# Larger score bursts, earlier transposes and an earlier block 1 in a fused attention and feed-forward kernel

## Chip, cores, metric

One NeuronCore of a Trainium2 chip. The metric is the device time of one execution in microseconds (us). The kernel before takes 245.7 us: 245.55 median of the 3 runs known when the prediction was made, 245.72 of 6 runs later.

## The reference

Sliding-window attention with a few global keys and a slope bias, then a gated feed-forward block on its output.

```python
batch, n_heads, seq, head_dim = (4, 8, 768, 64);  n_global, n_local = (8, 96)
scores = scale * (q @ k.T) + bias        # bias: -slope of the head x distance
scores = where(keep, scores, -1e9)       # keep: 8 global keys, or the 96 keys up to the query
a = softmax(scores);  x = (a @ v)        # heads side by side: 3072 tokens x 512
g = x @ w_gate                           # 512 x 1536
out = (g * sigmoid(g) * (x @ w_val)) @ w_out
```

## The kernel before

The 3072 tokens are 8 tiles of 384; block b (a batch entry) is tiles 2b and 2b + 1. The "head" of the program is what runs before the steps below; it does block 0's attention for its first 384 tokens, and "half 1", the other 384, is done during tile 0. The feed-forward work of a tile has 12 steps f. A step is a gate group (gps, 4 matmuls), a value group (vps, 4) and usually one output part (ops, 3 matmuls of the tile before; four parts make one output of 128 rows). Between the gate and value groups and the output stand a tanh (th, ScalarE) and two products (sl and hT, VectorE); an "eviction" is the copy of a finished output out of its PSUM bank. Attention work is slipped in between steps: score bursts (sc), transposes (trs), and values (den and num). TensorE writes PSUM, which has eight banks here: four (a0 to a3) for attention, three (x0 to x2) that gate and value groups take in turn, and o0 for outputs.

```python
def bank(name, dt=FP32):                       # the next of a0..a3
def spare(name, dt=FP32):                      # the next of x0..x2
    tag = state["x"][gv.get("n", 0) % len(state["x"])]
    gv["n"] = gv.get("n", 0) + 1
    return single(name, tag, dt)

def transposes_half(self, half, tr, k_eng, q_eng):      # of one pair of heads
    for st, dst in ((k16, trk), (q16, trq)):
        for j in range(J2):
            for hi in range(2):
                nc.tensor.transpose(dst[...], st[...], ident)
    ...                                         # then the copies out of PSUM (k_eng, q_eng)

def gate_or_val(t, f, which, c0=0):
    ...
    if which == 0:      # ScalarE: th = tanh(dst / 2);  VectorE: sl = (th + 1) * dst
    else:               # VectorE: hT = dst * sl

def out_part(t, i, part):
    ...                                         # 3 matmuls into o0
    if part == 3:
        nc.scalar.mul(out=osb, in_=ops, mul=0.5)            # the eviction of o0
        nc.sync.dma_start(out=out[r0:r0 + 128, :], in_=osb)

def sc(b, *units):                              # a burst: pairs (hp), thirds of the keys (bk)
    ...  pair.scores(bk, ..., [spare("sc") for _ in range(2)] if len(units) == 3 and i == 0
                     else banks("sc"))
# scores: matmuls now; the exponentials (ScalarE) of the first pair now, of the others "later";
# the masks (VectorE, for some GpSimd) later. One "later" item runs before each group.

def first(t, b):
    return {(t, 3): [tr(b, 0), tr(b, 1)],
            (t, 5): [sc(b, (0, 0), (0, 1), (1, 0))],
            (t, 7): [tr(b, 2), tr(b, 3)],
            (t, 8): [sc(b, (1, 1), (2, 0), (2, 1))],
            (t, 9): [sc(b, (3, 0), (3, 1))],
            (t, 10): [va(b, 0, 0)],
            (t, 11, 1): [va(b, 1, 0)]}

def both(t, b):
    n = b + 1
    return {(t, 0): [sc(b, (0, 2), (1, 2), (2, 2)), fetch(n, 0, 1)],
            (t, 5): [sc(b, (3, 2), (0, 0, n), (1, 0, n)), fetch(n, 2, 3)],
            (t, 8): [vas(b, 1)],
            (t + 1, 0): [sc(n, (0, 1), (1, 1), (2, 0))],
            (t + 1, 4): [sc(n, (2, 1), (3, 0), (3, 1))],
            (t + 1, 8): [vas(n, 0)]}

stretches = [                                   # ff(tile, first step, last step, output parts)
    (ff(0, 0, 12), half1),
    (ff(1, 0, 6, (0, 0, 0, 1, 0, 1)) + ff(1, 6, 11, (1,)) + [(1, 11, 5)], first(1, 1)),
    (ff(2, 0, 12, (1,)) + ff(3, 0, 12, (1,)), both(2, 1)),
    (ff(4, 0, 12, (1,)) + ff(5, 0, 12, (1,)), both(4, 2)),
    ...]
```

The softmax here doesn't subtract the row's maximum and nothing guards it: scores larger than these inputs give would overflow.

Of the kernel before, what the change touches and what calls it, by code (L numbers as in the profile page):

```python
# [37 lines left out]
def kernel(  # L38
# [223 lines left out]
    class Pair:  # L262
# [30 lines left out]
        def transposes_half(self, half, tr, k_eng, q_eng):  # L293
            hp = self.hp
            trq, trk = tr
            for st, dst in ((k16, trk), (q16, trq)):
                for j in range(J2):
                    for hi in range(2):
                        nc.tensor.transpose(  # L299
                            dst[64 * hi:64 * hi + 64, 128 * j:128 * j + 128],  # L300
                            st[:, half, 2 * hp + hi, D * j:D * j + D], ident)
            if half == 0:
# [62 lines left out]
        def scores(self, bk, mul_eng, put_off, sc):  # L365
# [30 lines left out]
            if put_off:  # L396
                later.append(exps)
            else:
                exps()
            later.append(mask)  # L400
# [11 lines left out]
    class Quad:  # L412
# [49 lines left out]
        def values(self, half, bank, mul_eng):  # L462
# [10 lines left out]
            def scale_num(side):  # L473
                mul_eng.tensor_mul(self.x_out(half, side), srcs[side], self.rb)  # L474

            def spread():
                self.spread()
                if mul_eng is nc.gpsimd:
                    for side in range(2):
                        scale_num(side)  # L480
# [3 lines left out]
            if mul_eng is not nc.gpsimd:  # L484
                for side in range(2):
                    later.append(lambda side=side: scale_num(side))
# [11 lines left out]
    def both_values(b, half):  # L498
# [23 lines left out]
        later.append(two[1].spread)  # L522
        for side in range(2):
            later.append(lambda side=side: scale_num(nc.vector, 1, side))
# [90 lines left out]
    def p_tr(hp, kt, qt, q_eng):  # L615
        tr = [single("trs", t, FP16)[:, 0:TB] for t in (qt, kt)]
        pairs[0, hp].transposes_half(0, tr, V, q_eng)
# [28 lines left out]
    load_qk(1, 4, 8)  # L646
    for c in range(NCH):
        load_v_rest(1, c)
# [28 lines left out]
    def sc(b, *units):  # L677
        def step():
            for i, (hp, bk, *other) in enumerate(units):
                pair = pairs[b + 1 if other else b, hp]  # L680
                on_vector = pair.b < 2 or bk < 2 or hp % 2 == 0
                pair.scores(bk, nc.vector if on_vector else nc.gpsimd, bool(later),
                            [spare("sc") for _ in range(2)] if len(units) == 3 and i == 0
                            else banks("sc"))
        return step

    def va(b, g, half):
        return lambda: quads[b, g].values(half, bank, nc.vector if b < 2 else nc.gpsimd)
# [7 lines left out]
    def trh(*units):  # L696
        def step():
            ks, qs = single("trs", "o0", FP16), spare("trs", FP16)
            for i, (hp, k_eng, q_eng) in enumerate(units):
                c = slice(TB * i, TB * i + TB)  # L700
                pairs[0, hp].transposes_half(1, [qs[:, c], ks[:, c]], k_eng, q_eng)
# [10 lines left out]
    def fetch(b, *hps):  # L712
        def step():
            for hp in hps:
                pairs[b, hp].transposes_dma()
            if hps[0] > 0:
                turn_ends(b)
        return step

    def first(t, b):  # L720
        return {(t, 3): [tr(b, 0), tr(b, 1)],
                (t, 5): [sc(b, (0, 0), (0, 1), (1, 0))],
                (t, 7): [tr(b, 2), tr(b, 3)],
                (t, 8): [sc(b, (1, 1), (2, 0), (2, 1))],
                (t, 9): [sc(b, (3, 0), (3, 1))],
                (t, 10): [va(b, 0, 0)],
                (t, 11, 1): [va(b, 1, 0)]}

    def both(t, b):

        n = b + 1
        return {(t, 0): [sc(b, (0, 2), (1, 2), (2, 2)), fetch(n, 0, 1)],
                (t, 5): [sc(b, (3, 2), (0, 0, n), (1, 0, n)), fetch(n, 2, 3)],
                (t, 8): [vas(b, 1)],
                (t + 1, 0): [sc(n, (0, 1), (1, 1), (2, 0))],
                (t + 1, 4): [sc(n, (2, 1), (3, 0), (3, 1))],
                (t + 1, 8): [vas(n, 0)]}
# [110 lines left out]
```

## Time and profile before

One profiled execution, cut where TensorE starts the head's first feed-forward matmul, tile 1's first gate group and tile 2's first value group. These starts are read from TensorE's order of time.

| stretch | us |
|---|---|
| start to the head's first feed-forward matmul (block 0's first half) | 15.41 |
| from there to tile 1's first gate group ("tile 0") | 27.97 |
| from there to tile 2's first value group ("tile 1") | 32.54 |
| from there to the end | 167.83 |
| sum | 243.75 |

Busy shares do not help: TensorE is busy 97% before and 96% after. What helps is the distance between starts: 0.65 us for an undisturbed group, and whatever is more is a burst, a mode change or a wait. In lines of the order of time the two numbers in front are start and duration, the brackets at the end hold the idle time before the first instruction and what ended it. A wait that ends before the modelled end of the matmul before it shows in the distance of the starts and not, or not fully, in the brackets.

### The profile page before, as it was taken

Reading aid. Unit: us, or ns where it says so; the run is one execution under the profiler, and the core shown is the slowest. Engines: PE = TensorE matmul, PEld = TensorE weight load, DVE = VectorE, ACT = ScalarE, POOL = GpSimd, SP = SyncE. Lnnn points to the kernel's source line nnn. Section 1 sums busy time; section 2 is a strip of 40 time slices with the busy share of each in tenths; the row PEclk is TensorE's granted clock in tenths of the full one; section 3 lists DMA queues with packets and bytes.
Section 4 is the critical chain, followed back from the end, with each engine's and each line's share of the span. In section 5 each row is a group of like instructions: output and inputs, shape, how many; then the busy total and the mean of one; then the engine's idle time right before and its main releaser. Section 6 shows DMA issues by size and latency. Waiting matters only on the chain.

```text
span 243.8 us, 6052 instructions
## 1 busy us (share of the span) xinstructions
PE 235.8 (97%) x2428; PEld 136.0 (56%) x2428; DVE 167.1 (69%) x358; ACT 129.4 (53%) x291; POOL 96.8 (40%) x117
## 2 busy tenths in 40 slices
PE   7899898999999999999999999999999999999994
PEld 4555565566465556555565556555655565555543
DVE  5676749888886768776786658776785568555510
ACT  6637576868763655356446465367346534333221
POOL 8999674738980000996062252800032213000000
PEclk9999999999999999999999999999999999999999
DMA  7999999999996684699309778951101101110122
GB/s 142 167 190 198 180 206 198 205 154 126 153 121 117 122 144 100 42 157 148 60 3 140 143 142 94 66 70 44 46 0 46 43 0 46 44 41 5 43 88 86
DMA packets 84612, 25.10 MB, mean 103 GB/s; under 512 B 72816, under 2 KB 81640, under 8 KB 84584
## 3 DMA queue, kind: packets, MB, share of 16 engines
q0 software_dynamic: 65296, 14.05, 65.9%
q1 hardware_dynamic: 18728, 10.30, 16.7%
q8 instruction: 19, 0.31, 0.6%
q10 hardware_dynamic: 560, 0.36, 0.5%
q14 instruction: 9, 0.07, 0.1%
HBM read 28.67 MB, written 6.29 MB: 143 GB/s over the span
## 4 chain that ended last, share of the span: by engine, by line
PE 84%; DVE 7%; ACT 3%; DMA 2%; issue 1%; POOL 0%; DVEq 0%; POOLq 0%
PE gps L539 24%; PE ops L568 23%; PE vps L539 23%; PE sc L375 3%; PE num L439 3%; DMA q<-in_q_dram 2%; PE den L439 2%; DVE sl L552 2%; DVE hT L556 2%; PE sc L335 2%; DVE xT L474 1%; ACT at L357 1%; PE trs L273 1%; ACT th L550 1%; PE trs L299 1%
## 5 line engine op out<-in xcount | busy, mean ns | idle before, releaser
L552 DVE SCALAR_TENSOR_TENSOR sl<-th,gps 128x384 f32<-128x384 f32 x94 | 52.0, 553 | 40.1 <-ACT th L550 39.1
L539 PE MATMUL gps<-xT,wg 128*128 128x384 f16 x376 | 76.9, 327 | 0.4
L539 PE MATMUL vps<-xT,wv 128*128 128x384 f16 x376 | 76.5, 326 | 0.6 <-DVE sl L552 0.5
L550 ACT ACTIVATE th<-gps 128x384 f32<-128x384 f32 x94 | 46.7, 497 | 53.5 <-PE gps L539 52.0
L568 PE MATMUL ops<-wo,hT 128*128 128x512 f16 x276 | 72.8, 379 | 0.0
L556 DVE TENSOR_TENSOR hT<-vps,sl 128x384 f16<-128x384 f32 x94 | 52.0, 554 | 7.9
L539 PEld LDWEIGHTS <-wg 128*128 128x128 f16 x384 | 35.1, 98 | 31.2 <-issue 2.3
L539 PEld LDWEIGHTS <-wv 128*128 128x128 f16 x384 | 37.5, 98 | 26.8 <-issue 2.1
L568 PEld LDWEIGHTS <-hT 128*128 128x128 f16 x276 | 26.9, 98 | 23.9
L383 ACT ACTIVATE at<-sc 128x432 f16<-128x432 f32 x72 | 33.1, 539 | 12.2 <-PE sc L375 12.2
L514 POOL TENSOR_TENSOR xT<-ns,rb 128x384 f16<-128x384 f32 x10 | 9.8, 997 | 67.5 <-DVE rb L455 56.5
L171 POOL DMA_DIRECT2D vS<-in_v_dram x28 | 24.7, 896 | 5.3 <-DMA kst<-in_k_dram 3.8
L574 ACT ACTIVATE osb<-ops 128x512 f32<-128x512 f32 x23 | 13.7, 597 | 21.9 <-PE ops L568 21.9
L394 POOL TENSOR_TENSOR at<-at,masks 128x864 f16<-128x864 f16 x4 | 7.3, 1822 | 23.8 <-ACT at L383 19.1
L394 DVE TENSOR_TENSOR at<-at,masks 128x864 f16<-128x864 f16 x20 | 12.1, 604 | 5.4 <-ACT at L383 5.4
L194 POOL DMA_DIRECT2D kst<-in_k_dram x16 | 13.9, 885 | 2.3 <-PE vps L539 1.7
L357 ACT ACTIVATE at<-sc 128x432 f16<-128x432 f32 (+2 forms) x32 | 11.7, 445 | 5.6 <-PE sc L346 5.4
L194 POOL DMA_DIRECT2D qst<-in_q_dram x16 | 13.7, 877 | 0.2 <-issue 0.2
L510 ACT COPY ns<-num 128x384 f32<-128x384 f32 x20 | 8.1, 492 | 7.9 <-PE num L439 7.9
L439 PE MATMUL num<-at,vS 128*32 128x216 f16 (+6 forms) x560 | 11.1, 226 | 0.0
L391 DVE TENSOR_TENSOR at<-at,masks 128x432 f16<-128x432 f16 x24 | 8.1, 378 | 4.1 <-ACT at L383 4.1
L449 DVE STREAM_TRANSPOSE dT<-den 128x384 f32<-128x384 f32 x16 | 9.3, 581 | 1.4 <-PE den L439 0.9
(74 smaller groups left out, 180.2 us busy)
## 6 DMA issues: line engine op xcount, KB each, us to landing
out_dram<-osb SPq DMA_DIRECT2D x23, 256.0 KB
vS<-in_v_dram POOLq DMA_DIRECT2D x24, 120.0 KB, 5.4
wo<-in_moe_w_out_dram POOLq DMA_DIRECT2D x4, 384.0 KB, 10.4
qst<-in_q_dram POOLq DMA_DIRECT2D x16, 96.0 KB, 4.3
kst<-in_k_dram POOLq DMA_DIRECT2D x16, 90.0 KB, 4.9
wg<-in_moe_w_gate_dram POOLq DMA_DIRECT2D x4, 256.0 KB, 7.7
wv<-in_moe_w_val_dram POOLq DMA_DIRECT2D x4, 256.0 KB, 7.7
kst<-in_k_dram POOLq DMA_DIRECT2D x2, 384.0 KB, 12.0
```

Of the source, the lines that this page charges most:

```text
L171: nc.gpsimd.dma_start(out=vSs[b][NG:NG + n, c, :, :], in_=v[b, :, KC * c:KC * c + n, :].rearrange("h p d -> p h d"))
L194: nc.gpsimd.dma_start(out=st[b][p0:p0 + n, h // 2, :, h % 2, :], in_=src[b, h, 0:n * J].rearrange("(t p) d -> p t d", p=n))
L357: nc.scalar.activation(out=at[:, hi, 0:col + n], in_=sc[hi][:, 0:col + n], func=AF.Exp, scale=scale)
L383: nc.scalar.activation(out=at[:, hi, :], in_=sc[hi][:, 0:BANK], func=AF.Exp, scale=scale)
L394: mul_eng.tensor_mul(at, at, m[:, :, o:o + BANK])
L439: nc.tensor.matmul(dst[r, o:o + n], lhsT=ones[:, 0:32] if side is None else vals[:, 4 * g + j, side::2], rhs=pairs[b, 2 * g + j // 2].at[c ...
L539: nc.tensor.matmul(gv[f, which][:, 0:TB], lhsT=w[:, c, 128 * f:128 * f + 128], rhs=x_of(t)[:, c, :], start=(c == 0), stop=(c == NC - 1))
L550: nc.scalar.activation(out=th, in_=dst[:, 0:TB], func=AF.Tanh, scale=0.5)
L552: nc.vector.scalar_tensor_tensor(out=sl, in0=th, scalar=1.0, in1=dst[:, 0:TB], op0=AluOp.add, op1=AluOp.mult)
L556: nc.vector.tensor_mul(hTs[t][:, f, :], dst[:, 0:TB], gv["sl"])
L568: nc.tensor.matmul(ops, lhsT=hTs[t][:, f, 128 * i:128 * i + 128], rhs=wo[:, f, :], start=(f == 0), stop=(f == NFF - 1))
L574: nc.scalar.mul(out=osb, in_=ops, mul=0.5)
```

## The change

Its intent is stated in its own words: "Score bursts of four pairs from the feed-forward banks on; half 1's transposes ahead of copies; two outputs ahead of tile 1; block 1's steps sooner". The core of the diff:

```diff
@@ trh: half 1 of block 0, two pairs at a time (cut)
-            for i, (hp, k_eng, q_eng) in enumerate(units):
-                pairs[0, hp].transposes_half(1, [qs[:, c], ks[:, c]], k_eng, q_eng)
+            for hp, tr in pair_of:
+                pairs[0, hp].turn_half(1, tr)
+            for hp, tr in pair_of:
+                pairs[0, hp].copy_half(1, tr, k_eng, A)
@@ sc: banks and order of the exponentials (cut)
+                where = ([spare("sc"), spare("sc")] if i == 0 and len(units) > 2 else
+                         [single("sc", "o0"), spare("sc")] if i == 3 else banks("sc"))
+            now = [0, 3] if len(units) == 4 else [0]
@@ values of half 1: one scaling to GpSimd
-        return lambda: quads[b, g].values(half, bank, nc.vector if b < 2 else nc.gpsimd)
+        return lambda: quads[b, g].values(half, bank, nc.gpsimd if (b, g, half) == (0, 1, 1) else nc.vector)
@@ first(t, b)
-        return {(t, 3): [tr(b, 0), tr(b, 1)],
-                (t, 5): [sc(b, (0, 0), (0, 1), (1, 0))],
-                (t, 7): [tr(b, 2), tr(b, 3)],
-                (t, 8): [sc(b, (1, 1), (2, 0), (2, 1))],
-                (t, 9): [sc(b, (3, 0), (3, 1))],
-                (t, 10): [va(b, 0, 0)],
-                (t, 11, 1): [va(b, 1, 0)]}
+        return {(t, 2): [tr(b, 0), tr(b, 1)],
+                (t, 3): [sc(b, (0, 0), (0, 1), (1, 0))],
+                (t, 5): [tr(b, 2), tr(b, 3)],
+                (t, 6): [sc(b, (1, 1), (2, 0), (2, 1))],
+                (t, 7): [sc(b, (3, 0), (3, 1))],
+                (t, 8): [va(b, 0, 0)],
+                (t, 10): [va(b, 1, 0)]}
@@ both(t, b)  (second is alike)
+        return {(t, 3): [all_of(b, 2), fetch(n)], (t, 7): [vas(b, 1)], (t, 11): [all_of(n, 0)],
+                (t + 1, 3): [all_of(n, 1)], (t + 1, 7): [vas(n, 0)]}
@@ stretches
-        (ff(0, 0, 12), half1),
-        (ff(1, 0, 6, (0, 0, 0, 1, 0, 1)) + ff(1, 6, 11, (1,)) + [(1, 11, 5)], first(1, 1)),
+        (ff(0, 0, 11) + [(0, 11, 2)], half1),
+        (ff(1, 0, 3) + ff(1, 3, 11, (1,)) + [(1, 11, 2)], first(1, 1)),
@@ loads of block 1: from the head to step 11 of tile 0
+    at_step(0, 11, lambda: load_qk(1, 4, 8), lambda: [load_v_rest(1, c) for c in range(NCH)])
```

Not shown here: at a tile's first step all "later" items were run at once, and now only those up to the last scaling are.

More of the change, by code (lines that the diff above doesn't have):

```diff
@@ L290, in transposes, with turn_half @@
                 in_=k3[:, 0, NG:2 * NG].unsqueeze(1).broadcast_to([128, NCH, NG]))
-        def transposes_half(self, half, tr, k_eng, q_eng):
+        def turn_half(self, half, tr):
             hp = self.hp
@@ L301, in transposes_half, with copy_half @@
                             st[:, half, 2 * hp + hi, D * j:D * j + D], ident)
+        def copy_half(self, half, tr, k_eng, q_eng):
+            trq, trk = tr
+            hp = self.hp
             if half == 0:
@@ L363, in scores_half, with scores @@
                 exps()
-        def scores(self, bk, mul_eng, put_off, sc):
+        def scores(self, bk, mul_eng, sc):
             hp = self.hp
@@ L394, in mask @@
                     mul_eng.tensor_mul(at, at, m[:, :, o:o + BANK])
-            if put_off:
-                later.append(exps)
-            else:
-                exps()
-            later.append(mask)
+            return exps, mask
         def transposes_dma(self):
@@ L473, in scale_num @@
             def scale_num(side):
-                mul_eng.tensor_mul(self.x_out(half, side), srcs[side], self.rb)
+                eng = mul_eng if side else nc.vector
+                eng.tensor_mul(self.x_out(half, side), srcs[side], self.rb)
             def spread():
@@ L478, in spread, with scale @@
                 if mul_eng is nc.gpsimd:
-                    for side in range(2):
-                        scale_num(side)
+                    scale_num(1)
             later.append(lambda: self.invert(den))
             later.append(spread)
-            if mul_eng is not nc.gpsimd:
-                for side in range(2):
-                    later.append(lambda side=side: scale_num(side))
+            for side in range(1 if mul_eng is nc.gpsimd else 2):
+                def scale(side=side):
+                    scale_num(side)
+                later.append(scale)
         def denominators(self, den):
@@ L521, in both_values, with spread, scale @@
         later.append(spread_first)
-        later.append(two[1].spread)
+        def spread():
+            two[1].spread()
+        later.append(spread)
         for side in range(2):
-            later.append(lambda side=side: scale_num(nc.vector, 1, side))
+            def scale(side=side):
+                scale_num(nc.vector, 1, side)
+            later.append(scale)
     hTs = {}
@@ L616, in p_tr @@
         tr = [single("trs", t, FP16)[:, 0:TB] for t in (qt, kt)]
-        pairs[0, hp].transposes_half(0, tr, V, q_eng)
+        pairs[0, hp].turn_half(0, tr)
+        pairs[0, hp].copy_half(0, tr, V, q_eng)
     V, A = nc.vector.tensor_copy, nc.scalar.copy
@@ L645 @@
     load_wo(3)
-    load_qk(1, 4, 8)
-    for c in range(NCH):
-        load_v_rest(1, c)
     p_bias(0, 0, "a0", "a1")
@@ L678, in step @@
         def step():
-            for i, (hp, bk, *other) in enumerate(units):
-                pair = pairs[b + 1 if other else b, hp]
-                on_vector = pair.b < 2 or bk < 2 or hp % 2 == 0
-                pair.scores(bk, nc.vector if on_vector else nc.gpsimd, bool(later),
-                            [spare("sc") for _ in range(2)] if len(units) == 3 and i == 0
-                            else banks("sc"))
+            work = []
+            for i, (hp, bk) in enumerate(units):
+                pair = pairs[b, hp]
+                on_vector = b < 2 or bk < 2 or hp % 2 == 0
+                where = ([spare("sc"), spare("sc")] if i == 0 and len(units) > 2 else
+                         [single("sc", "o0"), spare("sc")] if i == 3 else banks("sc"))
+                work.append(pair.scores(bk, nc.vector if on_vector else nc.gpsimd, where))
+            now = [0, 3] if len(units) == 4 else [0]
+            for i in now:
+                work[i][0]()
+            masks_now = [work[i][1] for i in now]
+            rest = [w for i, w in enumerate(work) if i not in now]
+            for exps, _ in rest:
+                later.extend(masks_now[:1] + [exps])
+                masks_now = masks_now[1:]
+            later.extend(masks_now + [mask for _, mask in rest])
         return step
     def va(b, g, half):
-        return lambda: quads[b, g].values(half, bank, nc.vector if b < 2 else nc.gpsimd)
+        return lambda: quads[b, g].values(half, bank, nc.gpsimd if (b, g, half) == (0, 1, 1) else nc.vector)
     def vas(b, half):
@@ L694, in tr, with trh @@
         return pairs[b, hp].transposes
-    def trh(*units):
+    def trh(h0, h1, by_engine):
         def step():
-            ks, qs = single("trs", "o0", FP16), spare("trs", FP16)
-            for i, (hp, k_eng, q_eng) in enumerate(units):
-                c = slice(TB * i, TB * i + TB)
-                pairs[0, hp].transposes_half(1, [qs[:, c], ks[:, c]], k_eng, q_eng)
+            b0, b1 = single("trs", "o0", FP16), spare("trs", FP16)
+            (a, b), (c, d) = [(t[:, 0:TB], t[:, TB:2 * TB]) for t in (b0, b1)]
+            k_eng = V if by_engine else A
+            pair_of = [(h0, (c, a)), (h1, (d, b))] if by_engine else [(h0, (b, a)), (h1, (d, c))]
+            for hp, tr in pair_of:
+                pairs[0, hp].turn_half(1, tr)
+            for hp, tr in pair_of:
+                pairs[0, hp].copy_half(1, tr, k_eng, A)
         return step
@@ L710, in sch, with fetch, all_of @@
         return step
-    def fetch(b, *hps):
+    def fetch(b):
         def step():
-            for hp in hps:
+            for hp in range(NP):
                 pairs[b, hp].transposes_dma()
-            if hps[0] > 0:
-                turn_ends(b)
+            turn_ends(b)
         return step
     def first(t, b):
-        return {(t, 3): [tr(b, 0), tr(b, 1)],
-                (t, 5): [sc(b, (0, 0), (0, 1), (1, 0))],
-                (t, 7): [tr(b, 2), tr(b, 3)],
-                (t, 8): [sc(b, (1, 1), (2, 0), (2, 1))],
-                (t, 9): [sc(b, (3, 0), (3, 1))],
-                (t, 10): [va(b, 0, 0)],
-                (t, 11, 1): [va(b, 1, 0)]}
+        return {(t, 2): [tr(b, 0), tr(b, 1)],
[5 more added lines that the diff above has]
+                (t, 10): [va(b, 1, 0)]}
+    def all_of(b, bk):
+        return sc(b, *[(hp, bk) for hp in range(NP)])
     def both(t, b):
         n = b + 1
-        return {(t, 0): [sc(b, (0, 2), (1, 2), (2, 2)), fetch(n, 0, 1)],
-                (t, 5): [sc(b, (3, 2), (0, 0, n), (1, 0, n)), fetch(n, 2, 3)],
-                (t, 8): [vas(b, 1)],
-                (t + 1, 0): [sc(n, (0, 1), (1, 1), (2, 0))],
-                (t + 1, 4): [sc(n, (2, 1), (3, 0), (3, 1))],
-                (t + 1, 8): [vas(n, 0)]}
+        return {(t, 3): [all_of(b, 2), fetch(n)], (t, 7): [vas(b, 1)], (t, 11): [all_of(n, 0)],
+                (t + 1, 3): [all_of(n, 1)], (t + 1, 7): [vas(n, 0)]}
     def second(t, b):
-        return {(t, 0): [sc(b, (0, 2), (1, 2))], (t, 3): [sc(b, (2, 2), (3, 2))],
-                (t, 7): [vas(b, 1)]}
-    half1 = {(0, 1): [trh((0, A, A), (1, V, A))], (0, 2): [sch(0)],
-             (0, 3): [sch(1), trh((2, V, A), (3, V, V))], (0, 5): [sch(2)], (0, 6): [sch(3)],
+        return {(t, 3): [all_of(b, 2)], (t, 7): [vas(b, 1)]}
+    half1 = {(0, 1): [trh(0, 1, False)], (0, 2): [sch(0)],
+             (0, 3): [sch(1), trh(2, 3, True)], (0, 5): [sch(2)], (0, 6): [sch(3)],
              (0, 7): [va(0, 0, 1)], (0, 8): [va(0, 1, 1)]}
@@ L793 @@
             if f == 0:
-                run_later(len(later))
+                while any(fn.__name__ in ("spread", "spread_first", "scale") for fn in later):
+                    run_later(1)
             for which in range(2):
```

## The prediction

> **What bounds the kernel now.** I read the page first (engine shares, then the chain that ended last), then the order of time of TensorE alone, then that of all engines around one burst.
>
> ```profile
> PE 235.8 (97%) x2428; PEld 136.0 (56%) x2428; DVE 167.1 (69%) x358; ACT 129.4 (53%) x291; POOL 96.8 (40%) x117
> ...
> PE 84%; DVE 7%; ACT 3%; DMA 2%; issue 1%; POOL 0%; DVEq 0%; POOLq 0%
> ```
>
> TensorE is the bound, but a modelled busy of 97% says nothing about pace, so I use start-to-start times. A gate group (gps), a value group (vps) and an output part (ops) each take 0.65 us when nothing is in the way. From 77 us to the end nearly every group keeps that pace: there only the bursts of attention work cost extra. Two bursts, from TensorE's order of time:
>
> ```profile
> 103.54 0.81 PE L568 MATMUL ops<-wo,hT 128*128 128x512 f16 x3
> 104.29 0.73 PE L375 MATMUL sc<-qT,kT 64*128 64x216 f16 x12
> 104.95 0.82 PE L539 MATMUL gps<-xT,wg 128*128 128x384 f16 x4
> ...
> 190.45 0.81 PE L568 MATMUL ops<-wo,hT 128*128 128x512 f16 x3
> 191.19 0.34 PE L375 MATMUL sc<-qT,kT 64*128 64x216 f16 x4
> ...
> 191.68 0.82 PE L539 MATMUL gps<-xT,wg 128*128 128x384 f16 x4
> ```
>
> From ops to the next gps is 1.41 us with three pairs in between and 1.23 us with two. Without the 0.65 of the ops itself, and with the 0.01 that the next group loses, a burst costs 0.77 or 0.58 us: 0.19 per pair, and 0.2 fixed for entering and leaving.
>
> The stalls lie in the first 77 us. Half 1 of block 0 (the same view):
>
> ```profile
> 18.69 0.36 PE L299 MATMUL trs<-ident,k 128*64 128x128 f16 x6
> ...
> 19.75 0.36 PE L299 MATMUL trs<-ident,k 128*64 128x128 f16 x6 [0.53 <-ACT kT L312]
> ...
> 20.42 0.82 PE L539 MATMUL gps<-xT,wg 128*128 128x384 f16 x4
> ...
> 26.54 0.36 PE L299 MATMUL trs<-ident,k 128*64 128x128 f16 x6 [0.77 <-DVE kT L312]
> ...
> 40.60 0.81 PE L539 MATMUL vps<-xT,wv 128*128 128x384 f16 x4 [0.46 <-DVE sl L552]
> 41.52 0.81 PE L539 MATMUL gps<-xT,wg 128*128 128x384 f16 x4
> 42.45 0.81 PE L539 MATMUL vps<-xT,wv 128*128 128x384 f16 x4
> 43.38 0.81 PE L539 MATMUL gps<-xT,wg 128*128 128x384 f16 x4
> ```
>
> The second pair's transposes wait for the first pair's copies, as both use the same two banks; at the end of tile 0 groups are 0.93 us apart instead of 0.65, because VectorE is busy without a gap from 35 to 43 us. In tile 1 the chain shows 1.70 us of ScalarE (exponentials) at 64.4, between two score bursts one step apart: TensorE goes from 64.38 (ops) to 66.44 (gps), 2.06 us for 0.65 + 0.58, so 0.83 us are lost. Tile 2's first gate group takes 0.95 us (74.98 to 75.93), so it waits 0.3 for its last input.
>
> **What the Trainium skill says.** "TensorEngine Tiling (Array Packing)", Key Properties: "Mode switching requires drain". The trace agrees: that is the fixed 0.2 us. "PSUM — Partial Sum Buffer", the specifications and the section on bank collisions: there are 8 banks, and engines are to be kept apart by bank; the trace shows the waits (0.53 and 0.77 above). "TensorE: Matmul & The Clock Gate", the paragraph on engine queue depths: ScalarE and VectorE are strict FIFO. The trace agrees: no ScalarE work here overtakes another. "ScalarE: Activation LUTs", What ACT_TABLE_LOAD costs: 186 ns + 0.833 ns per element, overlapping by some 93 ns. That gives 546 ns for 432 elements and 612 for 512; the trace has 539 and 597, and four exponentials start 0.41 us apart. I use the trace's.
>
> **The change part by part.**
>
> 1. *Fewer, larger bursts.* From tile 2 on there are 4 + 4 bursts of three pairs and 2 of two; after it 3 + 3 + 1 of four. Before: 8 x 0.77 + 2 x 0.58 = 7.32 us. After: 7 x (0.58 + 2 x 0.185 = 0.95) = 6.65. Gain **0.7**, all on TensorE's path.
>
> 2. *What it pays for that.* Four pairs take all eight banks: the three of gate and value, the four attention banks, and the output bank o0. The burst sits after f = 3 or 11, where the fourth output part has just ended, so ScalarE must first empty o0. All engines around the two-pair burst at 191.19 show what that takes:
>
> ```profile
> 191.29 0.60 ACT L574 ACTIVATE osb<-ops 128x512 f32<-128x512 f32 x1 [0.81 <-PE ops L568]
> ...
> 191.79 0.95 ACT L383 ACTIVATE at<-sc 128x432 f16<-128x432 f32 x2
> ```
>
> With B the burst's start, the eviction runs from B + 0.10 to B + 0.70, and the first pair's exponentials start at B + 0.60. The fourth pair would start at B + 3 x 0.185 = 0.555 and now waits for o0 until 0.74. The next gate group would start at B + 0.855, but its bank in the rotation of three is the first pair's, whose exponential ends at 0.60 + 0.54 = 1.14, so B + 1.18. Loss 1.18 - 0.855 = 0.32 us per burst, x 7 = **2.3 us**. Further on I find no wait: the tanh two steps later slips to about B + 4.3, sl ends at 5.4, and the bank is wanted at 5.7. In the kernel before no output eviction stands just ahead of a three-pair burst, and the next gate bank is one that VectorE frees.
>
> 3. *Transposes ahead of copies.* From 18.60 (the natural end before it) to gps 20.42 is 1.8 us for 24 transposes; 48 transposes in tile 1 run from 49.39 to 50.85, so 24 need 0.8. Gain 0.95 the first time. The second time (25.24 to 27.00) the same 0.95, but the tanh of that step then stands behind two query copies and two exponentials on ScalarE, and the value group after it waits some 0.6 for its bank. Together **1.35**.
>
> 4. *End of tile 0.* One scaling (546 ns, 0.46 from start to start) moves from VectorE to GpSimd, where it takes 997 ns and has time: GpSimd's loads of block 1 now come after it. Two output parts (1.3 us) go between tile 0's last value group and tile 1's first gate group. That last value group comes 1.35 sooner (41.10 for 42.45), the outputs end at 43.05, and tile 1 starts there instead of at 43.38, with 1.3 us of work already done: **1.6 us** ahead, part 3 included.
>
> 5. *Tile 1 sooner.* The work is the same less 1.3 us: 12 x 1.30 + 10 x 0.65 + two transposes of 1.55 + bursts 0.77 + 0.77 + 0.58 + values 2 x 1.0. But the transposes and the first burst are now one step apart instead of two, with mask exponentials on ScalarE in the same steps. Laid out by hand, the first burst waits 0.3 for the sl before it, the burst after the second transposes up to 0.9 (VectorE: two masks, two query copies of 0.95), the 0.83 between the two bursts stays, and tile 2's input comes about 0.75 late, as three output parts fewer cover it. That is 2.8 against 1.1 now, up to 1.7 worse. Such a layout adds up delays that partly fall on top of one another, so I take a fifth to a third of it: **+0.4**.
>
> Loads: the second half of block 1's keys and queries goes out some 3 us later (37.8 to about 41). The DMA queues are full until then and issues wait for earlier ones, so landing moves little: keys landed at 51.0 (37.82 + 13.2), queries at 53.6 (39.80 + 13.8), and they are wanted at about 55.5.
>
> Sum: -0.7 + 2.3 - 1.6 + 0.4 = +0.4, so 246.0. I shade it to **245.4**: the two waits of part 2 are the only large loss, each read from a single other burst, and a schedule that was tuned to end its outputs just before the burst may lose less than my layout says.
>
> **Rivals.** (a) The four-pair bursts are free: o0 and the exponentials come in time. For it: ScalarE is busy only 53%, and from 77 us on nothing waits today. Against: the eviction cannot start before B + 0.10 and takes 0.6. Then the sum is 245.55 - 0.7 - 1.6 + 0.4 = 243.6. (b) The head gains all it lost, without new waits in tile 1: about 3.3 us of stalls in tile 0 and 1.1 in tile 1 vanish, some 242.5 with the bursts free, 244 with them costing. Against: VectorE and ScalarE are the limit there and lose no work but one scaling. (c) ScalarE or VectorE becomes the bound in tile 1, with the full 1.7 us, or the later key loads hold up the second transposes: 247 to 248. For it: VectorE is at 80 to 90% in those slices; against: the average leaves room.
>
> **Range and chances.** The rivals span 242.5 to 248. I give 8 in 10 to 243.3 to 247.3. A gain of over 2% (below 240.6) would need more than all the stalls of the first 77 us, about 4.5 us, and the switches besides: 0.03. A loss of over 2% (above 250.5) would need both extra waits to be double what I find: 0.02. Within 2%: 0.95.
>
> **What would show each step right or wrong.** Part 1: seven score bursts after tile 2 starts, of 16 or 24 matmuls. Part 2: the gate group after each starts about 1.9 us after the ops before it; without the waits it would be 1.6. Its releaser is the exponential, that of the last pair's matmuls the output eviction. Part 3: no wait of transposes for copies; gps at 19.5 and 25.1 where it was 20.4 and 27.0. Part 4: tile 1's first gate group at about 43 with six output matmuls ahead of it. Part 5: waits of TensorE for VectorE and ScalarE between 50 and 75 us, and tile 2's start at 74 to 75.5. I am wrong by over 1 us if the bursts don't wait, or if tile 1 turns bound by ScalarE or VectorE, or waits for its loads.

## The result

The changed kernel takes 248.33 us (median of 6 runs, 247.88 to 249.57); the kernel before took 245.72 (6 runs). The ratio is 1.0104, with a 95% interval of 1.0062 to 1.0147. Ratios here are the mean time of one kernel's fast runs over that of the other's of the same rounds, so not quite the ratio of the medians quoted. The change is 1% slower; "within 2%" held, but the predicted time of 245.4 was 2.9 too low and 248.33 lies above the range.

The same four stretches (the head's first matmul is at 16.51 in this profile):

| stretch | before | after | difference | with the two output parts counted | predicted |
|---|---|---|---|---|---|
| start | 15.41 | 16.51 | +1.10 | | 0 |
| tile 0 | 27.97 | 29.10 | +1.13 | -0.17 (1.30 of outputs done already) | -1.6 |
| tile 1 | 32.54 | 32.80 | +0.26 | +1.56 (1.30 of outputs less) | +0.4 |
| tile 2 to the end | 167.83 | 169.38 | +1.55 | | +1.6 |

The stretch "start" is a difference between executions and not the change: block 0's first queries landed 0.8 us later in this execution, and later runs with the same head code started their feed-forward at 14.8 to 16.0 us. The profiled run was the slowest of its six (249.57). In tile 0 it is rather a lucky one: three further executions with the same code there (a1, a4 and e1 below) have +0.3 to +0.5 where it has -0.17. Without that line the stretches give +2.9, the timed runs +2.6.

The page of the changed kernel, engine shares and chain:

```profile
PE 238.4 (96%) x2428; PEld 137.1 (55%) x2428; DVE 165.1 (67%) x353; ACT 128.4 (52%) x295; POOL 97.5 (39%) x118
...
PE 77%; DMA 6%; ACT 6%; POOL 4%; DVE 4%; issue 2%; DVEq 0%; POOLq 0%
```

TensorE's share of the chain fell from 84% to 77%, and DMA rose from 2% to 6%: a new kind of wait. A four-pair burst with all engines beside it:

```profile
103.80 0.81 PE L576 MATMUL ops<-wo,hT 128*128 128x512 f16 x3
...
104.55 1.11 PE L379 MATMUL sc<-qT,kT 64*128 64x216 f16 x16
104.65 0.60 ACT L582 ACTIVATE osb<-ops 128x512 f32<-128x512 f32 x1 [0.81 <-PE ops L576]
105.14 1.79 ACT L387 ACTIVATE at<-sc 128x432 f16<-128x432 f32 x4
...
105.72 0.82 PE L547 MATMUL gps<-xT,wg 128*128 128x384 f16 x4
```

From the output group to the next gate group it is 1.92 us, the predicted figure, and all seven bursts take 1.91 to 1.93. The eviction starts 0.10 after the burst, and the gate group 1.17 after it (1.18 predicted). The view merges the four pairs; in a window that begins at 105.29 the fourth stands apart:

```profile
105.30 0.36 PE L379 MATMUL sc<-qT,kT 64*128 64x216 f16 x4
```

It starts 0.75 after the burst (0.74 predicted), although a pair takes only 0.19. The semaphores in the packed trace name the releasers that the prediction named: the eviction (osb) for this pair, the exponential (at) for the gate group.

Tile 0 in TensorE's order of time:

```profile
20.59 0.82 PE L547 MATMUL gps<-xT,wg 128*128 128x384 f16 x4
...
22.01 0.50 PE L547 MATMUL vps<-xT,wv 128*128 128x384 f16 x2 [0.28 <-DMA wv<-in_moe_w_val_dram]
...
28.57 0.50 PE L547 MATMUL vps<-xT,wv 128*128 128x384 f16 x2 [0.49 <-DMA wv<-in_moe_w_val_dram]
...
43.67 0.81 PE L547 MATMUL vps<-xT,wv 128*128 128x384 f16 x4 [0.77 <-DVE sl L560]
44.32 1.46 PE L576 MATMUL ops<-wo,hT 128*128 128x512 f16 x6
45.62 0.81 PE L547 MATMUL gps<-xT,wg 128*128 128x384 f16 x4
```

Step 2 (20.59, or 4.08 after the head's first matmul) is 0.93 sooner than before (5.01), as foreseen. But then two value groups wait in their middle for the weights wv (in the packed trace the last wv for steps 4 to 7 landed at 28.53). By step 5 only 0.50 us is left of the 1.46 that TensorE was ahead at step 4, and by step 9 still 0.52. The last value group of tile 0 waits 0.77 for VectorE: it starts 1.57 after its gate group (42.10), where the kernel before had 0.93.

And tile 1, in the same view:

```profile
56.51 0.81 PE L547 MATMUL vps<-xT,wv 128*128 128x384 f16 x4
58.19 0.81 PE L576 MATMUL ops<-wo,hT 128*128 128x512 f16 x3 [0.87 <-ACT osb L582]
...
77.79 0.79 PE L547 MATMUL gps<-xT,wg 128*128 128x384 f16 x2 [0.29 <-DVE xT L475]
```

The output group of step 5 waits for the eviction of the output before: it starts 1.68 after its value group at 56.51, so 1.03 is lost. ScalarE's order of time says why; the eviction stands behind four score exponentials and two mask exponentials:

```profile
55.15 0.37 ACT L252 ACTIVATE masks<-dist 128x216 f16<-128x216 f16 x1
55.42 0.94 ACT L387 ACTIVATE at<-sc 128x432 f16<-128x432 f32 x2
56.24 0.57 ACT L252 ACTIVATE masks<-dist 128x432 f16<-128x432 f16 x1
56.69 0.96 ACT L387 ACTIVATE at<-sc 128x432 f16<-128x432 f32 x2
57.51 0.63 ACT L582 ACTIVATE osb<-ops 128x512 f32<-128x512 f32 x1
```

### The profile page after: what moved, and what is told of

Its sections match the earlier page's. It is cut to its first block, busy times and chain, and to the rows that moved or that the text cites. A ratio compares the mean times of both kernels' runs of the same rounds, so it can differ in the third digit from the quotient of the medians.

```text
span 247.8 us, 6053 instructions
## 1 busy us (share of the span) xinstructions
PE 238.4 (96%) x2428; PEld 137.1 (55%) x2428; DVE 165.1 (67%) x353; ACT 128.4 (52%) x295; POOL 97.5 (39%) x118
## 4 chain that ended last, share of the span: by engine, by line
PE 77%; DMA 6%; ACT 6%; POOL 4%; DVE 4%; issue 2%; DVEq 0%; POOLq 0%
PE gps L547 23%; PE ops L576 23%; PE vps L547 22%; DMA wv<-in_moe_w_val_dram 4%; PE num L439 3%; DMA vS<-in_v_dram 3%; ACT at L387 2%; ACT osb L582 2%; PE den L439 2%; POOL k L119 1%; DVE xT L475 1%; POOL q L119 1%; PE trs L273 1%; POOL wg L213 1%; PE ops L592 1%
## 5 line engine op out<-in xcount | busy, mean ns | idle before, releaser
L558 ACT ACTIVATE th<-gps 128x384 f32<-128x384 f32 x94 | 47.6, 506 | 74.6 <-PE gps L547 73.7
L547 PEld LDWEIGHTS <-wg 128*128 128x128 f16 x384 | 35.6, 98 | 32.6 <-issue 1.7
L379 PE MATMUL sc<-qT,kT 64*128 64x216 f16 (+2 forms) x152 | 10.3, 247 | 0.4 <-ACT at L387 0.2
```

Of the source, the lines that this page charges most:

```text
L547: nc.tensor.matmul(gv[f, which][:, 0:TB], lhsT=w[:, c, 128 * f:128 * f + 128], rhs=x_of(t)[:, c, :], start=(c == 0), stop=(c == NC - 1))
L558: nc.scalar.activation(out=th, in_=dst[:, 0:TB], func=AF.Tanh, scale=0.5)
```

## The experiments

The theory after the result: three separate losses. From tile 2 on, each four-pair burst pays for the bank o0 and for the first exponential (+1.5). In tile 0 the weights land when they always did, so earlier transposes only find a new wait, and the scaling on GpSimd does not relieve VectorE. In tile 1 the eviction stands behind exponentials. The rivals are with each run. Twelve kernels ran, the first eleven timed in five rounds beside the kernel before. Stretches are from one profiled execution of each; "tile 0" counts from the head's first feed-forward matmul, so the start is left out. The kernels built on the changed one, and the run with two outputs ahead, do 1.30 us more of outputs in tile 0 and so much less in tile 1.

| run | median us | ratio to before (95%) | tile 0 | tile 1 | rest |
|---|---|---|---|---|---|
| before | 245.5 to 245.9 | | 27.97 | 32.54 | 167.83 |
| changed | 248.33 | 1.0104 (1.0062 to 1.0147) | 29.10 | 32.80 | 169.38 |
| a1, bursts of three | 247.17 | 1.0049 (1.0006 to 1.0092) | 29.54 | 32.81 | 167.83 |
| a2, no wait for weights | 248.00 | 1.0091 (1.0043 to 1.0140) | 28.59 | 32.81 | 169.36 |
| a3, scaling on VectorE | 247.94 | 1.0090 (1.0046 to 1.0134) | 29.30 | 32.82 | 169.37 |
| a4, masks later | 248.02 | 1.0085 (1.0045 to 1.0124) | 29.79 | 32.10 | 169.36 |
| b1, transposes ahead, alone | 245.46 | 0.9995 (0.9969 to 1.0020) | 27.17 | 32.54 | 167.81 |
| b2, with split weight load | 244.52 | 0.9965 (0.9940 to 0.9990) | 26.93 | 32.55 | 167.82 |
| c1, all mended | 245.65 | 1.0011 (0.9982 to 1.0040) | 27.94 | 32.10 | 167.84 |
| c2, outputs at the end | 244.91 | 0.9980 (0.9951 to 1.0008) | 28.74 | 31.73 | 167.82 |
| d1, b2 and two outputs ahead | 245.33 | 0.9985 (0.9943 to 1.0028) | 28.92 | 31.79 | 167.82 |
| d2, b2 and values first | 245.17 | 0.9965 (0.9931 to 1.0000) | 26.94 | 32.73 | 167.82 |
| d3, d2 and a copy on VectorE | 245.25 | 0.9966 (0.9932 to 1.0000) | 28.17 | 32.74 | 167.82 |
| e1, eviction twice | 253.51, one look | | 29.58 | 32.81 | 173.77 |

The last two stretches repeat to 0.02 us where the code is the same. Tile 0 does not: with the same code it is 29.1 to 29.8, as the weights land sooner or later. The intervals of the timed runs are 0.5 to 1% wide, so for single parts the stretches carry the argument and the timed runs only check its direction.

### a1: bursts of three again

```diff
 # on the changed kernel, from tile 2 on
-        return {(t, 3): [all_of(b, 2), fetch(n)], (t, 7): [vas(b, 1)], ...
+        return {(t, 0): [sc(b, (0, 2), (1, 2), (2, 2)), fetch(n, 0, 1)],
+                (t, 5): [sc(b, (3, 2), (0, 0, n), (1, 0, n)), fetch(n, 2, 3)], ...
```

> The changed kernel with the bursts of block 1's last third and of blocks 2 and 3 put back to three pairs (two in tile 6), at their old places; the rest of the change stays. Theory (each four-pair burst waits 0.19 us for the output eviction and 0.13 us for the first exponential): from tile 2 on the time falls by about 1.5 us, so some 246.8, and groups from tile 2's first value group to the end take 167.9 us again. Rival (the waits are covered, the loss is all in the first 77 us): no change beyond the run-to-run spread, 248.3.

The rest takes 167.83 us again, 1.55 less, to 0.01 as before, and the ratio falls from 1.0104 to 1.0049. The burst in TensorE's order of time:

```profile
104.76 0.81 PE L576 MATMUL ops<-wo,hT 128*128 128x512 f16 x3
...
106.17 0.82 PE L547 MATMUL gps<-xT,wg 128*128 128x384 f16 x4
```

It is 1.41 us for three pairs, against 1.92 for four. So a pair costs (1.41 - 0.65 + 0.01) / 3 = 0.26 us in a burst of three and (1.92 - 0.65) / 4 = 0.32 in one of four: the larger burst is the dearer one, although there are fewer changes between groups and bursts. This run puts back the places of the bursts with their size, so it doesn't separate the two.

### e1: the eviction made twice

```diff
 # on the changed kernel, for the output part just ahead of a four-pair burst
+            for _ in range(2 if gv.get("twice") else 1):
+                nc.scalar.mul(out=osb, in_=ops, mul=0.5)
```

> The changed kernel with the eviction of the output bank just ahead of each four-pair burst made twice (the same result written twice). Theory (part 2 of the prediction: the fourth pair waits for the output bank, and the next gate group for an exponential that stands behind the eviction): a second eviction starts 0.50 us after the first, so from the output group to the next gate group it takes 1.92 + 0.50 = 2.42 us, and from tile 2 on 7 x 0.5 = 3.5 us more than 169.4. Rival (the extra time of a burst is the array's own change of mode or its pace with eight banks): unchanged, 1.92 us.

All engines beside one burst:

```profile
103.98 0.81 PE L576 MATMUL ops<-wo,hT 128*128 128x512 f16 x3
...
106.10 0.36 PE L379 MATMUL sc<-qT,kT 64*128 64x216 f16 x4 [0.65 <-ACT osb L583]
...
106.53 0.82 PE L547 MATMUL gps<-xT,wg 128*128 128x384 f16 x4
```

The fourth pair now waits visibly for the eviction, and the distance is 2.55 us, 0.63 more than with one; the stretch grows by 4.39, which is 7 x 0.63. The expected 0.50 was too small, as the second of these two evictions, of the same bank into the same tile, started 0.63 after the first and not 0.50 (the pair of them took 1.23). With a1 this settles the burst: the eviction of o0 is on its path. The run delays the exponentials too, as they stand behind the eviction, so it doesn't share the 0.32 out between the two; the changed kernel's trace does (the fourth pair starts at 0.75, where it was worked out at 0.56 without the wait; the gate group at 1.17). (This was one look, its state unknown; the clock was 1.0 and only stretches are compared.)

### a2: no wait for weights

```diff
 # on the changed kernel; wrong results on purpose (relative error 0.51)
-                gv[f, which][:, 0:TB], lhsT=w[:, c, 128 * f:128 * f + 128],
+                gv[f, which][:, 0:TB], lhsT=w[:, c, 128 * (f % 2 if t == 0 else f):...],
```

> The changed kernel with wrong results on purpose: every step of tile 0 from the third on multiplies with the first two 128-column blocks of the gate and value weights, which landed long before; all loads are still made. Theory (the transposes put ahead of copies only bring TensorE sooner to weights that land when they always did): the waits for wv in tile 0 go, tile 0's sixth step starts about 1 us sooner (0.9 to 1.3), and the whole falls by 0.5 to 1.2, unless VectorE at the end of tile 0 takes it back. Rival (weights are no limit, the waits for wv are those of a late start of the profiled run): no gain.

The waits for wv are gone, and step 5 starts 11.00 us after the head's first matmul (12.40 in the changed kernel, 12.90 before): 1.40 sooner, a little over the expected 0.9 to 1.3. But TensorE's order of time has another wait a group later, one that the prediction had named (0.6):

```profile
28.00 0.81 PE L547 MATMUL vps<-xT,wv 128*128 128x384 f16 x4 [0.72 <-DVE sl L560]
```

At step 7 the gain over the kernel before is 17.74 - 16.70 = 1.04, where 1.35 was predicted; with the weights' waits, the changed kernel's own profile has 0.53 there, and those of a1, a3 and a4 have 0.09, -0.32 and -0.16. So the weights take 0.5 to 1.4 us of the step's gain. The expected 0.5 to 1.2 of the whole is not seen: the timed ratio, 1.0091, is too close to 1.0104 for a verdict of its own.

### b1 and b2: the transposes alone, and with a split load

```diff
 # b1: on the kernel before, only turn_half / copy_half and the new trh
-    half1 = {(0, 1): [trh((0, A, A), (1, V, A))], ...
+    half1 = {(0, 1): [trh(0, 1, False)], ...
 # b2: b1, and
-    load_w(4, 8)
+    load_w(4, 6)
+    load_w(6, 8)
```

> The kernel before with one part of the change alone: half 1's transposes of two pairs ahead of their copies. Counted from the first matmul of the head's feed-forward, tile 0's step 2 started at 5.01 us before. Theory (weights land when they always did): step 2 starts 0.94 sooner, then TensorE waits for wv and wg, and by step 5 (12.90 before) no more than 0.1 to 0.6 is left; the whole changes by less than 0.6. Rival (the prediction's part 3): step 5 and all after it are 1.35 sooner, 244.4.

> The same with the load of weight columns for steps 4 to 7 of tile 0 made in two halves (steps 4 and 5, then 6 and 7), so that what step 4 needs lands sooner. Theory: the waits for weights at step 4 shrink from 1 us to 0.3 or less, a wait of the value group of step 5 for VectorE's sl of some 0.6 appears instead, as in the run without weight waits; step 5 starts 0.9 to 1.6 sooner than before and the whole falls by 0.7 to 1.1 against the kernel before. Rival (the load path, not the order, is the limit): the same waits as in the run without the split.

In b1 the waits stand in TensorE's order of time for both weights:

```profile
25.73 0.50 PE L543 MATMUL gps<-xT,wg 128*128 128x384 f16 x2 [0.20 <-DMA wg<-in_moe_w_gate_dram]
...
27.13 0.50 PE L543 MATMUL vps<-xT,wv 128*128 128x384 f16 x2 [0.58 <-DMA wv<-in_moe_w_val_dram]
```

The value group's second half starts at 27.13 us, and in the other runs with earlier transposes and no split load at 27.3 to 28.8. In the kernel before it was due at 27.98 and did not wait: it came just behind its weights, which landed at 27.73 by the packed trace. In b1's profile 0.78 us were left at step 5, above the theory's 0.6, and 0.80 at tile 1; that execution was the fastest of its six. The timed runs show no gain (0.9995, interval -0.3 to +0.2%), which agrees with the theory's "less than 0.6" but would not exclude 0.7; the rival's 1.35 is outside.

In b2 both waits are gone, and the same wait for sl as in a2 is left:

```profile
27.76 0.81 PE L543 MATMUL vps<-xT,wv 128*128 128x384 f16 x4 [0.73 <-DVE sl L556]
```

What step 4 needs last landed at 24.80, where it landed at 27.09 in b1. Step 5 starts 1.90 sooner than before, more than the expected 0.9 to 1.6, and step 7 is at 16.69, within 0.01 of the run without any need for weights. So at step 4 the order of the loads was the limit and not the load path. For the whole of tile 0 that isn't shown: of the six kernels with the split load, c2, d1 and d3 waited for weights at other steps in their profiles (0.47 and 0.43; 0.80 and 0.35; 1.21 and 0.42). Tile 0 falls by 1.04, and the time by 0.35% (interval 0.1 to 0.6%): 244.52 us. This is the version that beats both kernels; d2 and d3, built on it, have the same ratio, with intervals that reach 1.

### a3: the scaling back on VectorE

```diff
-        return lambda: quads[b, g].values(half, bank, nc.gpsimd if (b, g, half) == (0, 1, 1) else nc.vector)
+        return lambda: quads[b, g].values(half, bank, nc.vector)
```

> The changed kernel with the one scaling of half 1 that went to GpSimd back on VectorE. Theory (both engines' scalings read two SBUF operands at the same time and VectorE's took 1.19 us instead of 0.54, so nothing was saved): the tail of tile 0 is as long as with GpSimd, within 0.2 us; VectorE's two scalings take 0.54 each. Rival (GpSimd relieves VectorE by 0.46 us, as predicted): 0.4 to 0.5 us slower.

Both sides missed: it is not equal, and the way round is the opposite of the rival. From step 11's gate group to tile 1's first gate group, two output parts included, the changed kernel takes 3.52 us (also in a1, a2 and a4, to 0.01), a3 takes 2.87. GpSimd's help costs 0.65. The two scalings of the changed kernel, all engines:

```profile
41.75 0.99 POOL L475 TENSOR_TENSOR xT<-ns,rb 128x384 f16<-128x384 f32 x1 [4.20 <-DVE rb L455]
41.97 1.19 DVE L475 TENSOR_TENSOR xT<-ns,rb 128x384 f16<-128x384 f32 x1
...
43.08 0.54 DVE L560 SCALAR_TENSOR_TENSOR sl<-th,gps 128x384 f32<-128x384 f32 x1
```

and of a3:

```profile
41.55 0.54 DVE L475 TENSOR_TENSOR xT<-ns,rb 128x384 f16<-128x384 f32 x1
...
42.01 0.54 DVE L560 SCALAR_TENSOR_TENSOR sl<-th,gps 128x384 f32<-128x384 f32 x1
...
42.47 0.55 DVE L475 TENSOR_TENSOR xT<-ns,rb 128x384 f16<-128x384 f32 x1
```

VectorE's scaling takes 1.19 us beside GpSimd's and 0.54 without it. It comes ahead of sl, which in a3 runs between the two scalings, so sl and the bank it frees are 0.65 later. The Trainium skill has this in "SBUF — State Buffer", Who interferes with whom: "A DVE instruction with two SBUF inputs contends with a GpSimd instruction that reads SBUF". The trace agrees, with the two durations above; the prediction had not looked there. In the timed runs a3 has 1.0090, which does not tell it from the changed kernel.

### a4: mask exponentials later

```diff
-    spots = [...] + [(1, f // 2) for f in range(10)]
+    spots = [...] + [(1, f) for f in (0, 0, 1, 1, 2, 2, 5, 5, 6, 6)]
```

> The changed kernel with the mask exponentials of the last pair moved on ScalarE from steps 3 and 4 of tile 1 to steps 5 and 6. Theory (in tile 1's step 5 the output group waits 1.03 us for an eviction that stands behind four score exponentials and two mask exponentials): the wait falls to 0.2 or less and the whole by 0.8 to 1.0. Rival (another wait takes its place, at the burst of step 6 or 7, where ScalarE is busy too): less than 0.3 gained.

The wait for the eviction in TensorE's order of time:

```profile
57.66 0.81 PE L576 MATMUL ops<-wo,hT 128*128 128x512 f16 x3 [0.16 <-ACT osb L582]
```

Its value group starts at 56.68, so 0.33 of the 1.03 is left (0.2 or less expected), and tile 1 takes 32.10 in place of 32.80. That is 0.70, just under the expected 0.8 to 1.0, and no other wait took its place. What still stands ahead of the eviction are the four score exponentials. The timed ratio (1.0085) agrees in direction only.

### c1 and c2: all mended together

```diff
 # c1: a1 + a3 + a4 + the split load of b2, on the changed kernel;  c2: c1, and
-        (ff(1, 0, 3) + ff(1, 3, 11, (1,)) + [(1, 11, 2)], first(1, 1)),
+        (ff(1, 0, 4) + ff(1, 4, 11, (1,)) + [(1, 11, 3)], first(1, 1)),
```

> The changed kernel with what the runs found mended together: bursts of three from tile 2 on (1.5), the scaling back on VectorE (0.6 at the end of tile 0), the last pair's mask exponentials later (0.7), the split weight load (0.5 to 0.9). If the losses add up: 248.3 - 3.3 to 3.7 = 244.6 to 245.0, so some 0.7 to 1.1 below the kernel before. Rival (they overlap): equal to the kernel before within 0.4.

> The same, with the output part after step 3 of tile 1 moved to the end of tile 1, so that three output parts and not two stand between tile 1's last value group and tile 2's first gate group. Theory: tile 2's first gate group waits 0.65 less for its input (0.76 in the changed kernel), and 0.5 to 0.6 comes off. Rival: VectorE is behind by then whatever TensorE does in between, or the burst of step 3 waits instead: no gain.

In c1 each mended stretch is there: 27.94, 32.10 and 167.84, together 0.46 less than before. From the changed kernel's profile the three stretches fall by 3.40, within the expected 3.3 to 3.7, so there the losses do add up. But the timed runs give 1.0011: the 0.7 to 1.1 below the kernel before is excluded, and the rival's "equal within 0.4" fits, though not for its reason, as no overlap is seen. The profiled execution was the fastest of c1's six; what the others lose is not shown. In c2, tile 1 falls by another 0.37 (0.5 to 0.6 expected): no wait for tile 2's input is left, but the burst of step 3 now waits 0.47 for sl, as its rival said. In this execution tile 0 again waited for weights (0.47 and 0.43), in spite of the split. Its 0.998 is not told from 1. What the changed kernel's plan for tile 1 costs shows here even when mended: 31.73 + 1.30 = 33.03 for the same outputs that take 32.54 before.

### d1: two outputs ahead of tile 1, alone

```diff
 # on b2
-        (ff(0, 0, 12), half1),
-        (ff(1, 0, 6, (0, 0, 0, 1, 0, 1)) + ...
+        (ff(0, 0, 11) + [(0, 11, 2)], half1),
+        (ff(1, 0, 6) + ...
```

> The kernel with the transposes ahead and the split weight load (on the order of the kernel before otherwise), and with one more part of the change: two output parts go ahead of tile 1, taken from its steps 3 and 5. Prediction's part 4 without the GpSimd scaling: the wait of some 0.3 us at tile 1's first gate group is filled, so tile 1's first gate group starts 1.0 later with 1.3 us of work done: 0.3 gained. Rival (what tile 1 loses as cover, its steps 3 to 5 then outrun ScalarE and VectorE): the 0.3 is given back or more, tile 1 to tile 2 takes more than 32.54 - 1.30 = 31.24 us.

From step 11 to tile 1's first gate group it takes 2.87 against 1.86 in b2: 1.01 for 1.30 us of work, so the predicted 0.3 is gained. Tile 1 takes 31.79, and 31.25 (b2's 32.55 less 1.30) would be even: 0.54 is given back, as the rival said. Tile 0's own 28.92 is not used here, because this execution waited 0.80 and 0.35 for weights. Against the changed kernel's 32.80 it also shows what the new plan of tile 1 costs: both have ten output parts in tile 1, and the old order takes 1.0 less. This is for block 1's earlier steps and the other places of the outputs together (five at the end of tile 1 in d1, two in the changed kernel).

### d2 and d3: the wait between the two score bursts of tile 1

```diff
 # d2: on b2
-                (t, 9): [sc(b, (3, 0), (3, 1))],
-                (t, 10): [va(b, 0, 0)],
+                (t, 9): [va(b, 0, 0)],
+                (t, 10): [sc(b, (3, 0), (3, 1))],
 # d3: d2, and half 1's last query copy on VectorE
-                pairs[0, hp].copy_half(1, tr, k_eng, A)
+                pairs[0, hp].copy_half(1, tr, k_eng, V if hp == 3 else A)
```

> The same kernel without that part, but in tile 1 the values of the first two pairs are weighed in step 9, between the two score bursts of steps 8 and 10, instead of after the second in step 10. Theory (the second burst waits 0.83 us because its banks are those of the first burst's exponentials, one step before): the wait goes, tile 1 to tile 2 takes about 31.7 instead of 32.54, and the whole is 0.7 to 0.9 below the kernel it is made from, some 243.8. Rival (the values need the same four banks and so wait as long, or the last values then wait for the last pair's masks): less than 0.3 gained.

> The same as the run with values first, and half 1's last query copy goes from ScalarE to VectorE, so that the tanh of tile 0's step 4 stands behind one copy less. Theory (the 0.73 us wait of step 5's value group is ScalarE's order): the wait falls by 0.3 to 0.45 and so does the whole. Rival (VectorE is then the later one): no gain or a loss up to 0.3.

In d2 the burst no longer waits, but the last values do, for the masks of the last pair:

```profile
71.15 0.48 PE L443 MATMUL den<-at,ones 128*32 128x144 f16 x6 [0.78 <-DVE at L395]
```

Tile 1 takes 32.73 (32.55 in b2): the rival was right, the wait only moved. In d3 the 0.73 wait for sl is replaced by 0.27 for the copy on VectorE; from step 4 to step 7 it takes 6.62 us for d2's 7.01, so 0.39 is gained, as expected. But the same profile waits 1.21 and 0.42 for the weights of step 8, and the timed ratio equals d2's (0.9966 and 0.9965). So 0.39 in tile 0 is either lost to the weights or too small to see; this stays open.

## Why the prediction was wrong, point by point

Two steps failed: parts 3 and 4 in tile 0, and the size of part 5 in tile 1. In tile 0 the last value group was to start 1.35 sooner, counted from the head's first feed-forward matmul, and started 0.12 later: 0.83 of that was gone by step 9 (part 3), 0.65 went at the end (part 4). Tile 1 took 1.56 more in place of 0.4.

- **Part 1, fewer bursts, and part 2, what they pay.** Right, in size and in cause. The sum was 2.3 - 0.7 = +1.6; 1.55 was measured, each burst took the predicted 1.92, putting three pairs back gave all of it back, and doubling the eviction lengthened each burst by the time of the second eviction.
- **Part 3, transposes ahead of copies.** This failed. The 0.95 per pair of transposes was right where TensorE waits for copies (0.93 at step 2; step 3 to step 4 takes 3.20 for 4.17). The step "together 1.35" assumed that nothing else was due by then. The weights for steps 2 to 7 were: 0.50 was left at step 5 in the profile, and a2 gives the value without them at step 7 as 1.04, so the tanh wait was also a little larger than the 0.6 stated (step 5 to step 7 takes 5.70 for the 4.84 of before, so 0.86). The prediction checked the landing of block 1's keys, which did not matter, and not that of the weights.
- **Part 4, GpSimd and the outputs ahead.** The outputs ahead gain 0.3, as said (d1). The scaling on GpSimd was to take 0.46 off VectorE, so that the last value group could keep the 1.35 (it is no term of its own in the sum); it costs 0.65. The prediction took GpSimd's 997 ns as free, because that engine was idle; it slows VectorE's own scaling by 0.65.
- **Part 5, tile 1 sooner.** The size was wrong: "a fifth to a third" of a worked 1.7, +0.4, where 1.56 was measured. The reason for the discount, that such delays fall on top of one another, did not hold. The terms were mixed: 0.83 between the bursts was right, 0.75 for tile 2's input was right (0.76: 77.01 to 78.42 is 1.41 for one group). The 0.3 and "up to 0.9" for the first burst and the one after the second transposes came out at 0.07 and 0.04. That the worked 1.7 is near the measured 1.56 is chance: some 1.1 of its terms did not come, and what came in their place was not in it. That is the 1.03 for the eviction behind exponentials (a4 gets 0.70 of it back), in the part of ScalarE's queue that had not been worked out for evictions.
- **What the skill was cited for.** That the fixed 0.2 of a burst is the drain at a change of mode is not shown: it comes from two bursts (0.77 and 0.58), and no run separates the change of mode from anything else.
- **The last step**, from 246.0 to 245.4, leaned on the hope that a tuned schedule loses less than a layout says. No run supports it: part 2, read from a single burst, was exact.
- **Rivals.** The one that came true is (c), "ScalarE or VectorE becomes the bound in tile 1, with the full 1.7 us", together with a tile 0 that gained almost nothing; the wait on ScalarE was an eviction's and not one that (c) had named. "The later key loads hold up the second transposes" did not happen: those waited for the eviction ahead of them.

What stays open: why the weights land later in some executions than in others, and how much they still cost with the split load: without the split, the value group's second half of step 4 started anywhere from 27.13 to 28.75 us, and step 5, counted from the head's first matmul, differs by 0.85 among a1, a3 and the changed kernel, whose code is the same until then. The spread is also why tile 0 alone has no sharp verdict in the timed runs.

## What to carry to other kernels

Before work is pulled forward, list everything that the pulled work needs next, loads above all: a wait that is removed from an engine that was just behind its data comes back as a wait for that data. A batch that takes the last free bank is tied to the slowest release of any of them; here a fourth pair cost 0.50 us where a pair in a batch of three cost 0.26. And a queue worked out for one consumer has to be worked out for every instruction in it, because the one that hurts is often the one that nobody was following.

## What the Trainium skill lacked or had wrong

- "SBUF — State Buffer", Who interferes with whom: right, and decisive here. From its "exclusive lock" one can expect the later of the two to wait, but it has no duration for two scalings of 128 x 384 from two SBUF inputs each: VectorE's, which started 0.22 after GpSimd's, took 1.19 us in place of 0.54, GpSimd's 0.99. The two side by side took 1.41, VectorE alone takes 2 x 0.54.
- "TensorEngine Tiling (Array Packing)", Key Properties: it says that a change of mode drains the array, but not what that costs. Here a burst of score matmuls costs 0.2 us beyond its pairs, an estimate from the bursts of two and three pairs (0.58 and 0.77), with whatever else there is in entering and leaving.
- "ScalarE: Activation LUTs", What ACT_TABLE_LOAD costs: durations agree (539 ns for an estimate of 546 by its figures, 597 for 612). The overlap of back-to-back instructions is 0.12 us for 432 elements (539 ns long, 0.417 from start to start), where the page has 0.093.
- "PSUM — Partial Sum Buffer": it says to evacuate promptly, but has no figure for two evictions of the same bank in a row: in e1 the second, into the same tile, started 0.63 us after the first, where an exponential starts 0.49 after an eviction. Whether the bank or the tile is the reason is not shown.
